# q and k of the first batch: loads by GpSimd's queue, with the cast to f16 in the transfer

## The chip, the cores and the metric

The kernel runs on one core of a Trainium2 chip. The metric is the device time of one execution in microseconds (us). The engines are named as the profile names them: PE is TensorE (PEld its weight loads), DVE is VectorE, ACT is ScalarE, POOL is GpSimd, and SP is SyncE, whose queue (SPq) issues nearly all transfers.

## What is computed

Sliding-window causal attention over 8 batches, 8 heads, 576 positions and 64 values a head, and behind it a gated MLP with a spatial mix. Cut to what matters:

```python
def _attn_ref(q, k, v):                       # each (8, 8, 576, 64), f32
    scores = scale * np.matmul(q, k.transpose(0, 1, 3, 2))
    mask = (rel >= 0) & (rel < window)        # window = 64, rel = row - column
    scores = np.where(mask, scores, -1000000000.0)
    attn = np.exp(scores - np.max(scores, axis=-1, keepdims=True))
    attn = attn / (np.sum(attn, axis=-1, keepdims=True) + 1e-09)
    return np.matmul(attn, v)
...
def _moe_ref(x, w_in, w_spatial, b_spatial, w_out):   # x: (8, 576, 512)
    h = np.maximum(x @ w_in, 0.0)
    u, v = h[..., :512], h[..., 512:]
    v_n = (v - mean(v)) / np.sqrt(var(v) + 1e-06)
    v_s = np.einsum('ts,bsd->btd', w_spatial, v_n) + b_spatial[None, :, None]
    return (u * v_s) @ w_out
```

## The kernel before, in words

**The order is written out.** All work is a list of named steps. The text ORDER gives for each step, in the order in which it is issued, its name, its engine and its buffers (`ck0_0:DVE:0` is step ck0_0, on VectorE, into buffer 0 of its kind). Each engine takes its steps in that order and waits only for the data and buffers of the step at its front. DQ is SyncE's queue. A planner's costs stand beside the steps in the code (`("DQ", 0.45)`), but the order no longer depends on them.

**Names.** A digit pair b_g is batch and group; a group is four of the eight heads. For each b and g:

- ldk, ldq (L412): load of k or q, 128 rows of 1152 f32 values (576 KB), by SyncE, into a buffer of kind "nat" (nk, nq in the profile).
- ck, cq (L416, carried out at L292, L295 or L300): the cast to f16 into a buffer of kind "hqk" (hk, hq), on ACT, DVE or POOL; POOL does it in three parts.
- tk, tq (L419): the transpose of that tile by VectorE, which gives kT and qT.
- S (L479): the scores on PE. E (L486): the exponential on ACT. M (L489): the mask, a minimum on DVE. Z and N, n (L502, L529, L531): sums and their inverse. P and X (L514, L522): attention times v, and the scaled result x.
- ldv (L433): v in five pieces per group, 128 positions of four heads each (128 KB, runs of 64 f32 values), by SyncE. cv: cast to f16 (hv); sl and su: copies shifted by 64 rows (hs). For batches 0 and 1 cv is in two parts: cv0_10 is batch 0, group 1, part 0, which needs the first two pieces of v of that group. sl0_10 and su0_10 copy its result.
- V, U, G, O and the steps around them: the MLP of a batch, which follows later. W are transposes of w_spatial on PE (L378), which use the identity id16.

**The head.** PE runs matmuls on a scratch tile (the D steps, L862) until there is work. On SyncE's queue the order at the start is ldb (the bias), ldk0_0, ldq0_0, ldk0_1, ldv0_00, ldq0_1, ldv0_10, ldv0_11, ldk1_0, ldv0_12, ldv0_13, ldv0_01, ldq1_0 and so on. The casts of batch 0 are ck0_0, cq0_0 and cq0_1 on VectorE and ck0_1 on ScalarE. On VectorE the order is ck0_0, tk0_0, cq0_0, tq0_0, tk0_1, cq0_1, tq0_1, sl0_10, M0_00, su0_10, M0_01, ck1_0.

**Setup ahead of the steps.** GpSimd makes keep (L244 to L247), from which VectorE makes the mask (L252 to L258, small copies), then the identity id16 (L250, a helper's two instructions), then one row of ones in each of two tiles vn4 (L264), which the spatial mix reads. Its first step of the list is cv0_10.

At the end of the kernel function a loop goes through the ordered list, gives each step its buffers and issues it:

Of the kernel before, what the change touches and what calls it, by code (L numbers as in the profile page):

```python
# [15 lines left out]
BIG = 65504.0  # L16

ORDER = """
D24:PE:0 ldb:DQ:0 D5:PE:1 D21:PE:2 ldk0_0:DQ:1 ck0_0:DVE:0 tk0_0:DVE:0 D18:PE:3 D2:PE:2 D14:PE:2
D19:PE:3 D10:PE:0 ldq0_0:DQ:2 ldk0_1:DQ:3 ldv0_00:DQ:0 ldq0_1:DQ:4 ldv0_10:DQ:1 D3:PE:3 ldv0_11:DQ  # L20
cv0_10:POOL:0 ldk1_0:DQ:5 ck0_1:ACT:1 ldv0_12:DQ ldv0_13:DQ ldv0_01:DQ cq0_0:DVE:2 ldq1_0:DQ:6
tq0_0:DVE:1 ldv0_02:DQ D1:PE:2 S0_0:PE:0:1 tk0_1:DVE:2 D22:PE:0 E0_01:ACT:0 E0_00:ACT:1 cq0_1:DVE:3
tq0_1:DVE:3 D15:PE:3 D6:PE:1 D0:PE:2 D26:PE:0 D23:PE:3 S0_r:PE:1:0 E0_r0:ACT:0 E0_r1:ACT cv0_11:POOL
sl0_10:DVE:0 M0_00:DVE ldv0_03:DQ su0_10:DVE M0_01:DVE ck1_0:DVE:0 M0_r:DVE D8:PE:1 Z0_00:PE:2
ldv0_04:DQ ldwin110:DQ:7 ldv0_14:DQ ldwin111:DQ ldwin100:DQ:1 S0_1:PE:1:0 N0_00:ACT:0 E0_11:ACT:2
# [144 lines left out]
class Plan:  # L170
# [3 lines left out]
    def add(self, name, engs, key, fn, deps=(), acq=(), uses=(), mode=None, nbytes=0, n=0):  # L174
        if isinstance(engs, tuple):
            engs = [engs]
        s = Step(name, engs, key, fn, deps, acq, uses, mode, nbytes, n)
        s.n = len(self.steps)
        self.steps.append(s)
        return s  # L180
# [20 lines left out]
def kernel(  # L201
# [11 lines left out]
    nc = tc.nc  # L213
# [19 lines left out]
    def bank(j):  # L233
        return SINGLE[j - 4][:, :]
# [12 lines left out]
    nc.gpsimd.affine_select(out=keep[:], in_=keep[:], compare_op=ALU.is_ge, fill=0.0,  # L247
                            base=64, channel_multiplier=-1, pattern=[[1, 64]])
    id16 = cpool.tile([128, 128], f16, name="id16")
    make_identity(nc, id16[:])  # L250
    mask = cpool.tile([128, 2, 8, 64], f16, name="mask")
    nc.vector.tensor_copy(mask[:, 0, 1, :], keep[:])  # L252
    nc.vector.tensor_scalar(mask[0:64, 0, 0, :], keep[0:64, :], -1.0, BIG, ALU.mult, ALU.add)
# [5 lines left out]
    NSB = 2  # L259
    mv_t = [cpool.tile([128, 5, 2], f32, name=f"mv{i}") for i in range(NSB)]  # L260
    vn4_t = [cpool.tile([65, 512], f16, name=f"vn4_{i}") for i in range(NSB)]
    for i in range(NSB):
        nc.vector.memset(mv_t[i][:], 1.0)
        nc.gpsimd.memset(vn4_t[i][64:65, :], 1.0)  # L264
    w_in_sb = [cpool.tile([128, 1024], f16, name=f"win{r}") for r in range(4)]
    w_out_sb = [cpool.tile([128, 512], f16, name=f"wout{r}") for r in range(4)]
    wspT = [cpool.tile([128, 576], f16, name=f"wspT{kk}") for kk in range(5)]
# [11 lines left out]
    def buf(tag, name):  # L279
        b = Buf(tag, name)  # L280
        if tag in SHAPES:
            shape, d = SHAPES[tag]
            b.make = lambda i: pool.tile(shape, d, tag=f"{tag}_{i}", bufs=1, name=name)
        return b

    plan = Plan()
    add = plan.add
    ENG = {"ACT": nc.scalar, "DVE": nc.vector, "POOL": nc.gpsimd, "PE": nc.tensor, "DQ": nc.sync}

    def cp(e, o, i):  # L290
        if e == "ACT":
            nc.scalar.copy(o, i)  # L292
        elif e == "POOL" and len(i.shape) == 2 and i.shape[1] > 1000:
            for n in (0, 384, 768):
                nc.gpsimd.tensor_copy(o[:, n:n + 384], i[:, n:n + 384])  # L295
        elif e == "POOL" and len(i.shape) == 4 and i.shape[1] > 2:
            for lo, hi in ((0, 2), (2, i.shape[1])):
                nc.gpsimd.tensor_copy(o[:, lo:hi, :, :], i[:, lo:hi, :, :])  # L298
        else:
            ENG[e].tensor_copy(o, i)  # L300

    def cost(n, a=True, d=True, p=True, d1=False):

        out = []
        if a:
            out.append(("ACT", 0.09 + 0.00083 * n))
        if d:
            out.append(("DVE", 0.07 + (0.00104 if d1 else 0.00053) * n))
        if p:
            out.append(("POOL", 0.14 + 0.00083 * n))  # L310
        return out
# [95 lines left out]
    def load_steps(b, g, key):  # L407
        early = b < 2

        def one(name, src, key):  # L410
            n = buf("nat", f"n{name}{b}_{g}")
            ld = add(f"ld{name}{b}_{g}", ("DQ", 0.45), key, lambda e: nc.sync.dma_start(  # L412
                n.t[:, :], src[b, 4 * g:4 * g + 4, :, :].rearrange("h (i j) d -> (h i) (j d)", j=18)),
                acq=[n], nbytes=1.57, n=128)
            h = buf("hqk", f"h{name}{b}_{g}")
            c = add(f"c{name}{b}_{g}", cost(1152), key,  # L416
                    lambda e: cp(e, h.t[:, :], n.t[:, :]), deps=[ld], acq=[h], uses=[n])
            qt = buf("qkT", f"{name}T{b}_{g}")
            d = add(f"t{name}{b}_{g}", ("DVE", 1.09), key, lambda e: nc.vector.transpose(  # L419
                qt.t[:, :].rearrange("p (i j) -> p j i", j=18),  # L420
                h.t[:, :].bitcast(f32).rearrange("p (j w) -> p j w", w=32)),
                deps=[c], acq=[qt], uses=[h])
            return qt, d

        KT[b, g], DKT[b, g] = one("k", k, key)
        QT[b, g], DQT[b, g] = one("q", q, key + 0.001)
        nv = buf("natv", f"nv{b}_{g}")
        lds = []
        for c in range(5):
            sn = 128 if c < 4 else 64  # L430
            lds.append(add(f"ldv{b}_{g}{c}", ("DQ", 0.42),
                           key + 0.002 + 0.0001 * c,
                           lambda e, c=c, sn=sn: nc.sync.dma_start(  # L433
                               nv.t[0:sn, c, :, :],
                               v[b, 4 * g:4 * g + 4, 128 * c:128 * c + sn, :].transpose([1, 0, 2])),
                           deps=lds[-1:], acq=[] if c else [nv], uses=[nv] if c else [],
                           nbytes=0.0051 * sn, n=4 * sn))
        hv = buf("hv", f"hv{b}_{g}")
        hs = buf("hs", f"hs{b}_{g}")
        parts = [(0, 2), (2, 4)] if early else [(0, 4)]  # L440
        done = []
        for n, (lo, hi) in enumerate(parts):
            w = hi - lo
            l0 = max(lo, 1)
            c = add(f"cv{b}_{g}{n}", cost(256 * w), key + 0.003,
                    lambda e, lo=lo, hi=hi: cp(e, hv.t[:, lo:hi, :, :], nv.t[:, lo:hi, :, :]),
                    deps=[lds[hi - 1]] + done[:1], acq=[hv] if n == 0 else [],
                    uses=[nv] + ([hv] if n else []))
            sl = add(f"sl{b}_{g}{n}", cost(256 * (hi - l0)), key + 0.0035,
                     lambda e, l0=l0, hi=hi: cp(e, hs.t[64:128, l0:hi, :, :], hv.t[0:64, l0:hi, :, :]),  # L450
                     deps=[c] + done[1:2], acq=[hs] if n == 0 else [],
                     uses=[hv] + ([hs] if n else []))
            su = add(f"su{b}_{g}{n}", cost(256 * w), key + 0.0035,
                     lambda e, lo=lo, hi=hi: cp(e, hs.t[0:64, lo + 1:hi + 1, :, :],
                                                hv.t[64:128, lo:hi, :, :]),
                     deps=[c, sl if n == 0 else done[1]], uses=[hv, hs])
            done += [c, sl, su]
        done.append(add(f"s4{b}_{g}", cost(256), key + 0.004, lambda e: cp(
            e, hs.t[64:128, 4, :, :], nv.t[0:64, 4, :, :]), deps=[lds[4], done[1]], uses=[nv, hs]))
        HV[b, g], HS[b, g] = hv, hs  # L460
        DHV[b, g] = done
# [417 lines left out]
    for s, eng, banks in CHOOSE(plan):  # L879
        for x in s.acq:  # L880
            if x.tag == "bank":
                x.t = bank(banks.pop(0))
            elif x.tag == "pair":
                x.t = PAIR[banks.pop(0)]
            else:
                x.t = x.make(banks.pop(0))
        s.fn(eng)


# [28 lines left out]
```

## Time and profile before

| | |
|---|---|
| timed runs | 195.65, 195.79, 197.39 us; median 195.79 |
| profiled execution | span 193.6 us from the first to the last instruction; its time outside the span is not listed, the median of the runs is 2.19 us longer |
| granted clock of PE | 1.000 |
| busy, share of the span | PE 95%, DVE 85%, ACT 81%, POOL 45% |
| moved by DMA | 42.73 MB; from HBM 32.79 MB read, to it 9.44 MB written |

How to read it: times in rows are microseconds from the start of the span. A row of a timeline gives the start, the length, the engine, the line of the code, the operation, the tile written and the tiles read with their shapes, a count, and in brackets how long the engine stood idle before it and what ended the wait. A transfer's row on SPq is the issuing alone; the bytes move later, and "DMA to landing" gives the time from the issue until its completion was seen.

### The profile page before, as it was taken

What the parts mean: (1) busy time and instruction counts of PE and PEld (TensorE: products, weight loads), DVE (VectorE), ACT (ScalarE), POOL (GpSimd) and SP (SyncE); (2) the same over time, 40 slices, a digit from 0 to 9 for tenths busy, and PEclk for the clock granted to TensorE, in tenths of its full rate; (3) what the DMA queues carried; (4) which work ended last, traced back from release to release, by engine and by line L of the source; (5) the groups of instructions that cost most, each with busy time, mean ns of one, the idle gap of its engine ahead of it and who ended that gap; (6) DMA issues with size and microseconds to landing.
All of it is one profiled execution on the core that took longest, in us unless ns stands there. A gap on an engine that the chain in (4) does not pass through costs nothing.

```text
span 193.6 us, 7606 instructions
## 1 busy us (share of the span) xinstructions
PE 184.9 (95%) x3218; PEld 107.0 (55%) x3218; DVE 163.7 (85%) x304; ACT 157.1 (81%) x282; POOL 87.4 (45%) x161
## 2 busy tenths in 40 slices
PE   7798998999999999999999999999999999999991
PEld 2352534556556664656665656565756565665560
DVE  4899899999999999998999999998996967468331
ACT  2269998998999999899979999999999875706430
POOL 4027775849932986701956577615641520000000
PEclk9999999999999999999999999999999999999999
DMA  5999999899989997619987999669958000600445
GB/s 177 373 316 290 391 355 333 168 275 373 242 205 332 261 335 179 149 38 289 367 230 184 310 310 282 196 177 218 306 125 266 22 3 0 224 30 0 135 166 191
DMA packets 50421, 42.73 MB, mean 221 GB/s; under 512 B 39377, under 2 KB 39761, under 8 KB 50386
## 3 DMA queue, kind: packets, MB, share of 16 engines
q1 hardware_dynamic: 50162, 42.04, 73.3%
q8 instruction: 25, 0.41, 0.9%
q10 hardware_dynamic: 224, 0.20, 0.3%
q14 instruction: 10, 0.08, 0.1%
HBM read 32.79 MB, written 9.44 MB: 218 GB/s over the span
## 4 chain that ended last, share of the span: by engine, by line
PE 70%; DVE 13%; ACT 9%; DMA 3%; issue 2%; SPq 1%
PE bank L617 50%; PE bank L614 4%; PE pair L479 4%; PE bank L514 3%; DMA nk<-in_k_dram 3%; PE bank L502 3%; ACT e L486 3%; DVE qT L419 2%; PE bank L702 2%; DVE e L489 2%; DVE kT L419 2%; DVE st L671 2%; DVE g L797 1%; DVE x L522 1%; ACT lz L529 1%
## 5 line engine op out<-in xcount | busy, mean ns | idle before, releaser
L617 PE MATMUL bank<-wspT,vn 128*64 128x512 f16 (+3 forms) x530 | 39.1, 296 | 0.0
L486 ACT ACTIVATE e<-pair 128x1024 f16<-128x1024 f32 x32 | 32.0, 1030 | 1.6 <-PE pair L479 1.4
L797 DVE TENSOR_TENSOR g<-bank,ru 128x512 f16<-128x512 f32 (+1 forms) x36 | 23.3, 654 | 9.4 <-PE bank L617 7.0
L647 ACT COPY ob<-bank 128x512 f32<-128x512 f32 (+1 forms) x38 | 21.9, 591 | 9.7 <-PE bank L617 8.4
L669 ACT ACTIVATE vs<-bank 128x512 f16<-128x512 f32 (+1 forms) x40 | 23.8, 602 | 7.1 <-PE bank L705 5.6
L617 PE MATMUL bank<-x,win 128*64 128x512 f16 (+2 forms) x304 | 29.1, 327 | 0.0
L617 PEld LDWEIGHTS <-vn 128*64 128x64 f16 (+1 forms) x530 | 20.8, 111 | 13.2 <-issue 0.2
L671 DVE BATCH_NORM_STATS2 st<-vs 128x6 f32<-128x512 f16 (+1 forms) x40 | 26.0, 670 | 2.3 <-ACT vs L669 2.2
L298 POOL COPY hs<-hv 64x512 f16<-64x512 f16 (+1 forms) x36 | 20.1, 585 | 16.3 <-ACT hv L292 8.4
L617 PE MATMUL bank<-win,x 128*64 128x512 f16 x216 | 27.0, 379 | 0.0
L617 PE MATMUL bank<-wout,g 128*64 128x512 f16 (+1 forms) x208 | 24.7, 371 | 0.0
L522 DVE TENSOR_TENSOR x<-bank,lz 128x512 f16<-128x512 f32 x32 | 21.2, 684 | 3.5 <-PE bank L514 2.2
L489 DVE TENSOR_TENSOR e<-e,mask 128x1024 f16<-128x1024 f16 x32 | 23.0, 725 | 0.5 <-ACT e L486 0.4
L763 ACT ACTIVATE ru<-bank 128x512 f32<-128x512 f32 (+1 forms) x38 | 21.6, 584 | 1.5 <-PE bank L617 0.8
L295 POOL CAST hk<-nk 128x384 f16<-128x384 f32 x36 | 19.4, 574 | 7.1 <-DMA nk<-in_k_dram 6.7
L529 ACT ACTIVATE lz<-bank 128x512 f32<-128x512 f32 x32 | 19.0, 599 | 1.9 <-PE bank L502 1.6
L298 POOL CAST hv<-nv 128x512 f16<-128x512 f32 x18 | 11.7, 661 | 18.8 <-DMA nv<-in_v_dram 18.7
L419 DVE STREAM_TRANSPOSE kT<-hk 128x576 f32<-128x576 f32 x16 | 19.9, 1241 | 0.2 <-ACT hk L292 0.2
L419 DVE STREAM_TRANSPOSE qT<-hq 128x576 f32<-128x576 f32 x16 | 19.8, 1237 | 0.2
L531 ACT ACTIVATE lz<-lz 128x512 f32<-128x512 f32 x32 | 19.6, 642 | 0.0
L295 POOL CAST hq<-nq 128x384 f16<-128x384 f32 x27 | 14.9, 588 | 10.3 <-DMA nq<-in_q_dram 7.8
L617 PEld LDWEIGHTS <-win 128*64 128x64 f16 x304 | 14.4, 110 | 9.2
(91 smaller groups left out, 298.9 us busy)
## 6 DMA issues: line engine op xcount, KB each, us to landing
nk<-in_k_dram SPq DMA_DIRECT2D x16, 576.0 KB, 6.6
nq<-in_q_dram SPq DMA_DIRECT2D x16, 576.0 KB, 6.1
nv<-in_v_dram SPq DMA_DIRECT2D x64, 128.0 KB, 5.9
out_dram<-ob SPq DMA_DIRECT2D x14, 512.0 KB, 5.8
wi<-in_moe_w_in_dram SPq DMA_DIRECT2D x8, 256.0 KB, 5.8
ws<-in_moe_w_spatial_dram SPq DMA_DIRECT2D x4, 288.0 KB, 7.6
nv<-in_v_dram SPq DMA_DIRECT2D x16, 64.0 KB, 4.5
wo<-in_moe_w_out_dram SPq DMA_DIRECT2D x4, 256.0 KB, 7.2
```

The lines of the kernel that those rows point to most:

```text
L295: nc.gpsimd.tensor_copy(o[:, n:n + 384], i[:, n:n + 384])
L298: nc.gpsimd.tensor_copy(o[:, lo:hi, :, :], i[:, lo:hi, :, :])
L419: d = add(f"t{name}{b}_{g}", ("DVE", 1.09), key, lambda e: nc.vector.transpose(qt.t[:, :].rearrange("p (i j) -> p j i", j=18), h.t[:, :].b ...
L486: ex = add(f"E{b}_{g}{u}", ("ACT", 0.91), key, lambda e, u=u: nc.scalar.activation(e2[u].t[:, :, :], sc[u].t[:, :, :], AF.Exp, bias=0.0, s ...
L489: mins.append(add(f"M{b}_{g}{u}", ("DVE", 0.65), key, lambda e, u=u: nc.vector.tensor_tensor(e2[u].t[:, :, :], e2[u].t[:, :, :], mask[:, : ...
L522: lambda e, u=u, ob=ob, lz=lz: nc.vector.tensor_tensor(x.t[:, u, :], ob.t[:, :], lz.t[:, :], ALU.mult),
L617: nc.tensor.matmul(o[c:c + 64, :], w[:, c:c + 64], x, start=start, stop=stop)
L647: lambda e: (nc.vector.tensor_copy if last else nc.scalar.copy)(view(), m.t[rows, 0:n]),
L669: rl = add(f"Vr{b}_{j}", ("ACT", 0.49), key, lambda e: nc.scalar.activation(vs.t[0:jn, :], m.t[0:jn, :], AF.Relu), deps=[pv], acq=[vs], us ...
L671: s1 = add(f"Vb{b}_{j}", ("DVE", 0.6), key + 0.02, lambda e: nc.vector.bn_stats(st6.t[0:jn, 0:6], vs.t[0:jn, :]), deps=[rl], acq=[st6], us ...
L763: lambda e, m=m, ru=ru, n=n: nc.scalar.activation(ru.t[:, 0:n], m.t[:, 0:n], AF.Relu), deps=[pu], acq=[ru], uses=[m])))
L797: nc.vector.tensor_tensor(g.t[:, 0:n], m.t[:, 0:n], ru.t[:, 0:n], ALU.mult)
```

## The change

The loads of q and k of batch 0 (four of 576 KB) move from SyncE's queue to GpSimd's, and write f16 straight into the "hqk" tiles: the cast is part of the transfer. The four cast steps of batch 0 and their f32 buffers are gone. In ORDER the four loads stand at the front (k of group 0, q of group 0, k of group 1, q of group 1). GpSimd's identity and its two memsets of vn4 are issued behind the fourth of them instead of ahead of the list; keep stays ahead. The order of all other steps is as before.

```diff
--- before.py
+++ after.py
@@ -16,10 +16,10 @@
 BIG = 65504.0
 
 ORDER = """
-D24:PE:0 ldb:DQ:0 D5:PE:1 D21:PE:2 ldk0_0:DQ:1 ck0_0:DVE:0 tk0_0:DVE:0 D18:PE:3 D2:PE:2 D14:PE:2
-D19:PE:3 D10:PE:0 ldq0_0:DQ:2 ldk0_1:DQ:3 ldv0_00:DQ:0 ldq0_1:DQ:4 ldv0_10:DQ:1 D3:PE:3 ldv0_11:DQ
-cv0_10:POOL:0 ldk1_0:DQ:5 ck0_1:ACT:1 ldv0_12:DQ ldv0_13:DQ ldv0_01:DQ cq0_0:DVE:2 ldq1_0:DQ:6
-tq0_0:DVE:1 ldv0_02:DQ D1:PE:2 S0_0:PE:0:1 tk0_1:DVE:2 D22:PE:0 E0_01:ACT:0 E0_00:ACT:1 cq0_1:DVE:3
+D24:PE:0 ldk0_0:POOL:0 ldq0_0:POOL:2 ldk0_1:POOL:1 ldq0_1:POOL:3 ldb:DQ:0 D5:PE:1 D21:PE:2 tk0_0:DVE:0 D18:PE:3 D2:PE:2 D14:PE:2
+D19:PE:3 D10:PE:0 ldv0_00:DQ:0 ldv0_10:DQ:1 D3:PE:3 ldv0_11:DQ
+cv0_10:POOL:0 ldk1_0:DQ:5 ldv0_12:DQ ldv0_13:DQ ldv0_01:DQ ldq1_0:DQ:6
+tq0_0:DVE:1 ldv0_02:DQ D1:PE:2 S0_0:PE:0:1 tk0_1:DVE:2 D22:PE:0 E0_01:ACT:0 E0_00:ACT:1 
 tq0_1:DVE:3 D15:PE:3 D6:PE:1 D0:PE:2 D26:PE:0 D23:PE:3 S0_r:PE:1:0 E0_r0:ACT:0 E0_r1:ACT cv0_11:POOL
 sl0_10:DVE:0 M0_00:DVE ldv0_03:DQ su0_10:DVE M0_01:DVE ck1_0:DVE:0 M0_r:DVE D8:PE:1 Z0_00:PE:2
 ldv0_04:DQ ldwin110:DQ:7 ldv0_14:DQ ldwin111:DQ ldwin100:DQ:1 S0_1:PE:1:0 N0_00:ACT:0 E0_11:ACT:2
@@ -247,7 +247,6 @@
     nc.gpsimd.affine_select(out=keep[:], in_=keep[:], compare_op=ALU.is_ge, fill=0.0,
                             base=64, channel_multiplier=-1, pattern=[[1, 64]])
     id16 = cpool.tile([128, 128], f16, name="id16")
-    make_identity(nc, id16[:])
     mask = cpool.tile([128, 2, 8, 64], f16, name="mask")
     nc.vector.tensor_copy(mask[:, 0, 1, :], keep[:])
     nc.vector.tensor_scalar(mask[0:64, 0, 0, :], keep[0:64, :], -1.0, BIG, ALU.mult, ALU.add)
@@ -261,7 +260,6 @@
     vn4_t = [cpool.tile([65, 512], f16, name=f"vn4_{i}") for i in range(NSB)]
     for i in range(NSB):
         nc.vector.memset(mv_t[i][:], 1.0)
-        nc.gpsimd.memset(vn4_t[i][64:65, :], 1.0)
     w_in_sb = [cpool.tile([128, 1024], f16, name=f"win{r}") for r in range(4)]
     w_out_sb = [cpool.tile([128, 512], f16, name=f"wout{r}") for r in range(4)]
     wspT = [cpool.tile([128, 576], f16, name=f"wspT{kk}") for kk in range(5)]
@@ -408,13 +406,17 @@
         early = b < 2
 
         def one(name, src, key):
-            n = buf("nat", f"n{name}{b}_{g}")
-            ld = add(f"ld{name}{b}_{g}", ("DQ", 0.45), key, lambda e: nc.sync.dma_start(
-                n.t[:, :], src[b, 4 * g:4 * g + 4, :, :].rearrange("h (i j) d -> (h i) (j d)", j=18)),
-                acq=[n], nbytes=1.57, n=128)
+            view = src[b, 4 * g:4 * g + 4, :, :].rearrange("h (i j) d -> (h i) (j d)", j=18)
             h = buf("hqk", f"h{name}{b}_{g}")
-            c = add(f"c{name}{b}_{g}", cost(1152), key,
-                    lambda e: cp(e, h.t[:, :], n.t[:, :]), deps=[ld], acq=[h], uses=[n])
+            if b == 0:
+                c = add(f"ld{name}{b}_{g}", ("POOL", 1.0), key,
+                        lambda e: nc.gpsimd.dma_start(h.t[:, :], view), acq=[h], nbytes=1.57, n=128)
+            else:
+                n = buf("nat", f"n{name}{b}_{g}")
+                ld = add(f"ld{name}{b}_{g}", ("DQ", 0.45), key, lambda e: nc.sync.dma_start(
+                    n.t[:, :], view), acq=[n], nbytes=1.57, n=128)
+                c = add(f"c{name}{b}_{g}", cost(1152), key,
+                        lambda e: cp(e, h.t[:, :], n.t[:, :]), deps=[ld], acq=[h], uses=[n])
             qt = buf("qkT", f"{name}T{b}_{g}")
             d = add(f"t{name}{b}_{g}", ("DVE", 1.09), key, lambda e: nc.vector.transpose(
                 qt.t[:, :].rearrange("p (i j) -> p j i", j=18),
@@ -885,6 +887,10 @@
             else:
                 x.t = x.make(banks.pop(0))
         s.fn(eng)
+        if s.name == "ldq0_1":
+            make_identity(nc, id16[:])
+            for i in range(NSB):
+                nc.gpsimd.memset(vn4_t[i][64:65, :], 1.0)
 
 
 # ---- launch: one core; inputs and outputs as the reference has them ----
```

## The prediction

> **What bounds the kernel now.** I read the page first, then the windows, the chain of waits, and the timelines of VectorE, SyncE's queue and GpSimd in the first 14 us. The page gives the length:
>
> ```profile
> span 193.6 us, 7606 instructions
> ```
>
> The timed runs have a median of 195.79 us; 2.19 us of that lie around the span, and I add them unchanged. The windows view has the stretch, busy us of PE, PEld, DVE, ACT and POOL (instructions), the granted clock, the busy share of the DMA engines and their GB/s:
>
> ```profile
> 2.00:3.00 1.00, 1.00 (x4) 0.34 (x3) 0.92 (x4) 0.09 (x1) 0.94 (x3) 1.00 0.76 161
> 3.00:4.20 1.20, 1.20 (x4) 0.39 (x3) 0.57 (x4) 0.00 (x0) 0.17 (x1) 1.00 0.98 361
> 4.20:5.66 1.46, 1.46 (x5) 0.59 (x4) 0.40 (x1) 0.00 (x0) 0.00 (x0) 1.00 1.01 395
> 5.66:7.18 1.52, 1.52 (x8) 0.61 (x6) 1.49 (x3) 0.00 (x0) 0.00 (x0) 1.00 1.00 387
> 7.18:9.10 1.92, 0.96 (x5) 0.32 (x4) 1.89 (x3) 0.90 (x1) 0.00 (x0) 1.00 1.08 382
> 9.10:9.95 0.85, 0.69 (x57) 0.65 (x57) 0.67 (x2) 0.25 (x1) 0.00 (x0) 1.00 1.34 309
> 12.55:33.41 20.86, 19.01 (x366) 9.08 (x365) 19.58 (x33) 18.67 (x35) 14.56 (x22) 1.00 1.08 340
> 33.41:193.60 160.19, 155.75 (x2760) 93.41 (x2759) 134.99 (x252) 134.04 (x245) 69.91 (x127) 1.00 0.69 200
> ```
>
> From 33.41 us on TensorE is busy 155.75 of 160.19 us, and from 12.55 to 33.41 us VectorE is busy 19.58 of 20.86 us. So what the head loses or gains arrives at the end nearly whole, and the head alone is changed. In the head the DMA engines are the limit: from 3.00 us their share is about 1.0. The bytes say what passes when. A q or k load is 0.59 MB; 161 x 1.00 + 361 x 1.20 is 0.594 MB, so k of group 0 has passed at 4.20 us. 395 x 1.46 (0.577) brings q of group 0 at 5.66, 387 x 1.52 (0.588) k of group 1 at 7.18, 382 x 1.92 (0.733) one 0.131 MB piece of v and q of group 1 at 9.10, and 309 x 0.85 (0.263) the next two pieces of v at 9.95. Their order is that of SyncE's queue:
>
> ```profile
> 1.21 0.38 SPq L412 DMA_DIRECT2D nk<-in_k_dram  x1
> 1.63 0.43 SPq L412 DMA_DIRECT2D nq<-in_q_dram  x1
> 2.10 0.43 SPq L412 DMA_DIRECT2D nk<-in_k_dram  x1
> 2.57 0.43 SPq L433 DMA_DIRECT2D nv<-in_v_dram  x1
> 3.05 0.92 SPq L412 DMA_DIRECT2D nq<-in_q_dram  x1
> 4.01 1.12 SPq L433 DMA_DIRECT2D nv<-in_v_dram  x2
> ```
>
> The tiles' answers for the first loads of k and of q give the time from issue to landing:
>
> ```profile
> DMA to landing us min/median/max: 4.0/5.1/6.1
> ```
>
> ```profile
> DMA to landing us min/median/max: 5.0/6.1/7.2
> ```
>
> k lands at 1.21 + 4.0 = 5.21 and 2.10 + 6.1 = 8.20, q at 1.63 + 5.0 = 6.63 and 3.05 + 7.2 = 10.25: 1.0 to 1.15 us after the last byte passed. The chain of waits goes through the second k:
>
> ```profile
> 2.10 6.08 DMA nk<-in_k_dram
> 8.18 0.02 issue
> 8.20 1.16 ACT hk L292
> ```
>
> and then through VectorE's timeline:
>
> ```profile
> 5.26 0.76 DVE L300 CAST hk<-nk 128x1152 f16<-128x1152 f32 x1 [1.66 <-DMA nk<-in_k_dram]
> 6.06 1.26 DVE L419 STREAM_TRANSPOSE kT<-hk 128x576 f32<-128x576 f32 x1
> 7.16 0.75 DVE L300 CAST hq<-nq 128x1152 f16<-128x1152 f32 x1
> 7.95 1.26 DVE L419 STREAM_TRANSPOSE qT<-hq 128x576 f32<-128x576 f32 x1
> 9.38 1.26 DVE L419 STREAM_TRANSPOSE kT<-hk 128x576 f32<-128x576 f32 x1 [0.18 <-ACT hk L292]
> 10.49 0.74 DVE L300 CAST hq<-nq 128x1152 f16<-128x1152 f32 x1
> 11.27 1.26 DVE L419 STREAM_TRANSPOSE qT<-hq 128x576 f32<-128x576 f32 x1
> 12.55 0.22 DVE L300 COPY hs<-hv 64x256 f16<-64x256 f16 x1
> 12.81 0.69 DVE L489 TENSOR_TENSOR e<-e,mask 128x1024 f16<-128x1024 f16 x1
> ```
>
> The reader is to see two things. The four transposes end at 12.53 and everything on VectorE follows without a gap. And the next instruction, the copy hs (step sl0_10), stands ahead of the first mask step M0_00, though it needs v and not q or k.
>
> **The change part by part.** GpSimd's timeline:
>
> ```profile
> 1.34 0.24 POOL L247 TENSOR_SCALAR_AFFINE_SELECT keep<-keep 128x64 f16<-128x64 f16 x1
> 1.52 0.20 POOL masks.py:197 MEMSET id<- 128x128 f16 x1
> 1.79 0.29 POOL masks.py:199 TENSOR_SCALAR_AFFINE_SELECT id<-id 128x128 f16<-128x128 f16 x1
> 2.14 1.03 POOL L264 MEMSET vn<- 1x512 f16 x2
> 11.50 0.61 POOL L300 CAST hv<-nv 128x512 f16<-128x512 f32 x1 [8.33 <-DMA nv<-in_v_dram]
> ```
>
> *Moved setup.* The identity and the two memsets (1.52 to 3.17, so 1.65 us) go behind four transfers. They cost nothing: GpSimd idles 8.33 us before the cast of v at 11.50, and the identity's first reader is late:
>
> ```profile
> 35.48 2.39 PE L378 MATMUL bank<-id,wn 128*128 128x128 f16 x25
> ```
>
> Without that cover they would cost their 1.65 us. VectorE's mask waits for keep, which stays in front.
>
> *Issuing by GpSimd.* No row shows it. Below it is bounded by SyncE's 0.38 us for the same load; above by one pass of GpSimd over such a tile, three casts:
>
> ```profile
> 17.10 1.90 POOL L295 CAST hq<-nq 128x384 f16<-128x384 f32 x3 [1.02 <-DVE e L489]
> ```
>
> I take 1.0 us, near the middle, which is also what the diff enters for the planner. Keep is done at 1.58, so the four issues end at 2.6, 3.6, 4.6 and 5.6. SyncE's first k was issued by 1.59 and its bytes begin at 2.0, 0.4 later; so GpSimd's bytes begin at 3.0, not at 2.0. The Trainium skill, DMA: Bandwidth & Descriptors, section Latency and other measured facts, gives the first byte as about 1 us on GpSimd's path and 0.6 us on SyncE's; with that extra 0.4 us in place of my 1.0 the loads would begin at 2.4 and nothing below would change, because v decides.
>
> *SyncE's queue loses four loads.* The v pieces, behind three or four 0.59 MB loads until now, come first. The DMA engines have the same bytes to move and stay full: in 2.0 to 3.0 the 0.161 MB that k had now go to v.
>
> *Sharing.* From 3.0 on two queues feed the same engines. I take one row of k or q (4608 B) in turn with one packet of v (256 B, one head of one position), at the 385 GB/s of the middle rows: k and q get 4608 of 4864 parts, 365 GB/s, 1.62 us a load, and pass at 4.62, 6.24, 7.86 and 9.48. The other ends, SyncE's queue getting nothing or half, are 1.53 and 3.06 us a load. Landed, with 1.0, 1.0, 1.0 and 1.15 us: 5.62, 7.24, 8.86, 10.63.
>
> *Casts removed.* They go from VectorE (0.76, 0.75, 0.74) and ScalarE (1.16). The transposes then run 5.62 to 6.88, 7.24 to 8.50, 8.86 to 10.12 and 10.63 to 11.89 instead of ending at 12.53: 0.64 us earlier. The first scores start near 8.5 instead of:
>
> ```profile
> 9.26 0.67 PE L479 MATMUL pair<-qT,kT 32*128 32x128 f16 x56 [1.12 <-DVE qT L419]
> ```
>
> *What is late next: v.* hs needs the cast at 11.50, which waits for the second piece of v of group 1, the third piece in all. Of 0.393 MB, 0.161 pass by 3.0, 0.131 in turn with the 32 rows per engine, and the last 0.101 at 309 GB/s in 0.33 us: 9.81 instead of 9.95. With the lag of before (11.50 - 9.95 = 1.55) the cast starts at 11.36, ends at 11.97, and hs starts at about 12.0 instead of 12.55. Behind hs on VectorE stands M0_00, behind that on TensorE the sums and the next scores, and behind those ScalarE's work. So of 1.76 us of casts on the chain (1.16, and 0.60 between 10.64 and 11.24) only 0.55 us come out.
>
> **Sum:** 195.79 - 0.55 = 195.24, say 195.2 us (span 193.0). Its own range is 194.4 to 196.2.
>
> **The rivals.** *GpSimd's issuing is late.* The loads hold the gain as long as the last lands by 12.53 - 1.26 = 11.27; with an issue of g, 1.58 + 4g + 0.4 + 1.62 + 1.15 passes that at g = 1.63. At 1.90 it lands at 12.35 and the transposes end at 13.61, 1.08 us late: 196.9. A second way there is that VectorE's mask copies hold GpSimd off:
>
> ```profile
> 2.75 0.49 DVE L257 COPY mask<-mask 128x192 f16<-128x192 f16 x1
> 3.27 0.29 DVE L258 COPY mask<-mask 128x512 f16<-128x512 f16 x1
> ```
>
> The smaller copy, while GpSimd's memsets ran (2.14 to 3.17), took 0.49 us and the larger one, alone, 0.29: the two engines do disturb each other. If the first issue starts only at 3.56, the bytes begin at 4.96, the four loads pass at 11.44, land at 12.6, and the transposes end at 13.85: 1.3 us late, 197.1. Against it: the copies have gaps, and end at 3.56. The Trainium skill, SBUF — State Buffer, section Who interferes with whom, states this as a rule: a VectorE copy in a two-port mode blocks GpSimd wholly, and with it the writing of descriptors. By that rule the time is the 197.1; the stretched copy agrees with a disturbance, not with its size.
>
> *Equal shares in bytes* (the rival on the other side). If SyncE's queue, filled with v and the next batch's k, gets half of 385 GB/s, a load takes 3.06 us, the fourth passes at 15.26, lands at 16.4 and the transposes end at 17.7, 5.1 us late: 200.9. It turns slower once the four loads need more than 11.27 - 1.15 - 3.0 = 7.1 us, under 332 GB/s, 86% of the engines. For it: SyncE's queue holds 4608 B rows too, behind the v pieces. Against: 96 small v packets per engine come before them, and the four loads have 32 rows per engine. The Trainium skill, DMA: Bandwidth & Descriptors, section Queues, rings and completion order, has the engines change between queues packet by packet; read on one-row packets that is my sum, read on packets filled to equal size it is this rival. No row of before can tell, since one queue did all.
>
> *The cast halves the transfer's rate.* Same price, 200.9; nothing in the trace shows a cast in a transfer, and the change would then remove casts from idle engines to slow the bound one.
>
> *The whole saving.* If v passes early and a load that writes half its bytes costs the engines less, all 1.76 us come out: 194.0. It needs the fourth load by 9.5 us. Against it: 0.59 MB are still read, and the share is 1.0 already.
>
> **How the numbers follow.** Forecast 0.50, late issuing 0.18, equal shares 0.12, a slow cast 0.06, the whole saving 0.14. The range reaches up over late issuing and the milder forms of unequal sharing to 199.0, which leaves out about 0.12, and down to 194.0, which leaves out about 0.07. A measurement of this kernel tells about 1% (1.96 us) from no change. Faster by that, under 193.8: half of the whole saving and a little of the forecast's tail and of luck behind the head, 0.11. Slower, over 197.75: both heavy cases and a tail of the third, 0.21. Between: 0.68.
>
> **What would show it.** Right: a GpSimd queue with four issues near 1.0 us from about 1.6; no casts of hk and hq before 14 us; first scores at 8.3 to 8.9; the last transpose before 12.0; hs waiting for GpSimd's cast of v and starting near 12.0; the same 0.5 us at 33 us and at the end. Wrong: the fourth load landing after 11.3 us (late issuing if its issue is late, sharing or a slow cast if its bytes are), v landing well before 11, or a head gain that is gone at the end.

## The result and the profile after

| | before | after |
|---|---|---|
| median of 15 runs each, us | 195.81 | 197.54 |
| ratio, 95% interval | | 1.007 (1.0042 to 1.0098) |
| span of the profiled execution, us | 193.6 | 195.7 |
| landings of k0, q0, k1, q1 (digit: group), us | 5.2, 6.6, 8.2, 10.25 | 6.8, 8.3, 11.2, 12.8 |
| last transpose ends, hs starts, us | 12.53, 12.55 | 14.09, 14.11 |

The change is slower by 0.7%; the forecast was 195.2 us. The ratio is not the quotient of the medians, which would be 1.009: the means of the runs, 196.06 us before and 197.45 after, are 1.39 us apart, the medians 1.73 us. From the page of the changed kernel, the span, and the new queue with its packets, MB and share of the engines:

```profile
span 195.7 us, 7605 instructions
...
q0 software_dynamic: 576, 1.18, 3.2%
```

The four loads are 576 packets, 144 each (128 rows and 16 more), and are counted at the 1.18 MB they write, half of what they read. GpSimd's timeline:

```profile
1.52 0.67 POOL L413 DMA_DIRECT2D hk<-in_k_dram  x1
2.19 0.54 POOL L413 DMA_DIRECT2D hq<-in_q_dram  x1
2.71 0.59 POOL L413 DMA_DIRECT2D hk<-in_k_dram  x1
3.29 0.54 POOL L413 DMA_DIRECT2D hq<-in_q_dram  x1
...
11.92 0.61 POOL L298 CAST hv<-nv 128x512 f16<-128x512 f32 x1 [6.47 <-DMA nv<-in_v_dram]
```

The issues take little more than half of what was assumed and are over at 3.83. SyncE, free of four loads, begins to issue v at 1.23, ahead of GpSimd's first load, and issues the next batch's k at 2.78, ahead of GpSimd's fourth:

```profile
1.23 1.51 SPq L435 DMA_DIRECT2D nv<-in_v_dram  x3
2.78 0.52 SPq L416 DMA_DIRECT2D nk<-in_k_dram  x1
```

From issue to landing, first for hk and then for hq (minimum, median, maximum of two loads of each after the change):

```profile
DMA to landing us min/median/max: 5.3/6.9/8.5
```

```profile
DMA to landing us min/median/max: 6.1/7.8/9.5
```

So k lands at 1.52 + 5.3 = 6.8 and 2.71 + 8.5 = 11.2, q at 2.19 + 6.1 = 8.3 and 3.29 + 9.5 = 12.8. The windows view, with three of the prediction's windows:

```profile
2.00:3.00 1.00, 1.00 (x4) 0.35 (x3) 0.88 (x5) 0.10 (x1) 1.00 (x3) 1.00 0.54 123
3.00:4.20 1.20, 1.20 (x4) 0.41 (x3) 0.21 (x3) 0.00 (x0) 1.12 (x4) 1.00 0.65 116
5.66:7.18 1.52, 1.52 (x6) 0.56 (x5) 0.29 (x1) 0.00 (x0) 0.00 (x0) 1.00 1.06 195
```

Before, the share of the DMA engines was 0.76 from 2.00 to 3.00 and 0.98 from 3.00 to 4.20; now it is 0.54 and 0.65. Then it is full, and GB/s reads low only because cast rows count at half. VectorE's timeline has none of batch 0's casts left, and in their place four waits for transfers:

```profile
6.89 1.26 DVE L421 STREAM_TRANSPOSE kT<-hk 128x576 f32<-128x576 f32 x1 [3.68 <-DMA hk<-in_k_dram]
8.35 1.26 DVE L421 STREAM_TRANSPOSE qT<-hq 128x576 f32<-128x576 f32 x1 [0.20 <-DMA hq<-in_q_dram]
11.26 1.25 DVE L421 STREAM_TRANSPOSE kT<-hk 128x576 f32<-128x576 f32 x1 [1.65 <-DMA hk<-in_k_dram]
12.83 1.26 DVE L421 STREAM_TRANSPOSE qT<-hq 128x576 f32<-128x576 f32 x1 [0.31 <-DMA hq<-in_q_dram]
14.11 0.22 DVE L298 COPY hs<-hv 64x256 f16<-64x256 f16 x1
14.37 0.69 DVE L491 TENSOR_TENSOR e<-e,mask 128x1024 f16<-128x1024 f16 x1
```

The chain of waits names the fourth load:

```profile
3.29 9.51 DMA hq<-in_q_dram
12.80 0.02 issue
12.83 1.27 DVE qT L421
```

hs starts 1.56 us later than before. At 33 us the same sums on TensorE start 1.70 us later, first before the change, then after it:

```profile
33.41 0.41 PE L502 MATMUL bank<-e,ones 128*64 128x512 f16 x2 [0.24 <-DVE e L489]
...
35.11 0.41 PE L504 MATMUL bank<-e,ones 128*64 128x512 f16 x2 [0.24 <-DVE e L491]
```

The median is 1.73 us longer. The loss is made by 14 us and kept.

### The profile page after: what moved, and what is told of

Its sections match the earlier page's. It is cut to its first block, busy times and chain, and to the rows that moved or that the text cites. A ratio compares the mean times of both kernels' runs of the same rounds, so it can differ in the third digit from the quotient of the medians.

```text
span 195.7 us, 7605 instructions
## 1 busy us (share of the span) xinstructions
PE 185.5 (95%) x3218; PEld 107.2 (55%) x3218; DVE 161.0 (82%) x301; ACT 155.9 (80%) x281; POOL 92.2 (47%) x165
## 3 DMA queue, kind: packets, MB, share of 16 engines
q0 software_dynamic: 576, 1.18, 3.2%
## 4 chain that ended last, share of the span: by engine, by line
PE 78%; ACT 7%; DVE 5%; DMA 5%; issue 1%; POOL 1%; POOLq 0%
PE bank L619 53%; PE bank L616 8%; DMA hq<-in_q_dram 5%; PE pair L481 4%; PE bank L516 4%; PE bank L504 3%; ACT e L488 3%; PE bank L704 3%; DVE st L673 1%; ACT hs L290 1%; DVE qT L421 1%; ACT lz L533 1%; ACT lz L531 1%; PE bank L376 1%; DVE e L491 1%
## 5 line engine op out<-in xcount | busy, mean ns | idle before, releaser
L491 DVE TENSOR_TENSOR e<-e,mask 128x1024 f16<-128x1024 f16 x32 | 24.7, 776 | 0.3 <-ACT e L488 0.3
L293 POOL CAST hk<-nk 128x384 f16<-128x384 f32 x36 | 20.5, 604 | 4.5 <-DMA nk<-in_k_dram 4.3
```

The lines of the kernel that those rows point to most:

```text
L491: mins.append(add(f"M{b}_{g}{u}", ("DVE", 0.65), key, lambda e, u=u: nc.vector.tensor_tensor(e2[u].t[:, :, :], e2[u].t[:, :, :], mask[:, : ...
```

## The experiments

The theory formed from these traces: **the four loads lost their place.** In one queue the order of issue is a priority; in two queues v and the next k of SyncE share the engines with q and k of batch 0. The rivals: the cast makes the transfer slow; GpSimd issues late or is held off by VectorE's copies; the moved setup costs. Each experiment was compared with the kernel before on the same chip.

### The four loads alone: e1_gate and e5_gate_nocast

SyncE's queue is held behind a small copy out of the fourth tile, so the four loads have the engines to themselves; e5 does the same with f32 loads and the casts on chip. So v comes late in both, and what is read is the landings, not the times.

```diff
-... ldq0_1:POOL:3 ldb:DQ:0 D5:PE:1 ...
+... ldq0_1:POOL:3 ldb:DQ:0 gate:DQ:9 D5:PE:1 ...
+    add("gate", ("DQ", 0.4), -1.0, lambda e: nc.sync.dma_start(
+        gt.t[:, 0:256], GATED["q", 1].t[:, 0:256]), acq=[gt])
```

> The changed kernel, but SyncE issues nothing behind the bias until q of group 1 has landed (a small copy of that tile on its queue waits for it), so GpSimd's four loads have the DMA engines to themselves; the whole time is not the point, since v comes late. Landings of k0, q0, k1, q1 were 6.8, 8.3, 11.2 and 12.8 us in the changed kernel. Sharing (SyncE's packets slow the four loads): 5.6 to 6.0, then 1.5 us apart, the fourth by 10.5. GpSimd's path itself (late first bytes, late completions): the first still at 6.4 to 6.8, then 1.5 apart or more, the fourth at 11.2 to 12. A slow cast: 2 us or more apart even alone, the fourth at 12.5 or later.

> The first experiment (SyncE held until q of group 1 has landed) with f32 loads and the casts on chip: the four loads alone on the engines, without the cast. So far the fourth landed at 10.6 us alone with the cast, 12.8 shared with it, 11.4 shared without it. If the cast costs engine time by itself, the fourth lands at about 9.2 (10.6 less the 1.4 of the shared pair) and the spacing shrinks. If the cast costs only in turn with SyncE's packets, it lands at 10.2 to 10.6 as with the cast. The whole time tells nothing.

Landing of hq in e1 (the 2.0 is the gate's own copy), then of nq in e5 (1.9 is the gate):

```profile
DMA to landing us min/median/max: 2.0/5.1/7.3
```

```profile
DMA to landing us min/median/max: 1.9/5.1/7.0
```

In e1 the fourth load lands at 3.29 + 7.3 = 10.6, where the prediction had it (10.63) with v beside it; in e5 at 3.23 + 7.0 = 10.2. Alone, neither GpSimd's queue nor the cast is slow: the cast costs 0.4 us in four loads (one execution of each) and does not halve the rate. The times, 200.21 and 200.68 us (one run each), hold v's delay (hs waits until 16.36 and 15.86) and a stretch of half clock (last section).

### With sharing, without the cast: e2_nocast

```diff
-ldk0_0:POOL:0 ldq0_0:POOL:2 ldk0_1:POOL:1 ldq0_1:POOL:3 ...
+ldk0_0:POOL:1 ldq0_0:POOL:2 ldk0_1:POOL:3 ldq0_1:POOL:4 ...   (f32, into "nat")
+ck0_0:DVE:0 ... ck0_1:ACT:1 ... cq0_0:DVE:2 ... cq0_1:DVE:3   (as before)
```

> The changed kernel with f32 loads by GpSimd's queue and the four casts back on VectorE and ScalarE: the queue alone is changed, not the cast. Sharing and GpSimd's path both expect the same landings as in the changed kernel within 0.4 us (6.8, 8.3, 11.2, 12.8), the last transpose at about 15.6 instead of 14.1 us, and about 199.0 us. A slow cast expects the fourth landing at 11.8 or earlier and about 198 us or less.

Measured 199.89 us, ratio 1.0183 (1.0151 to 1.0215). Landing of nq:

```profile
DMA to landing us min/median/max: 6.1/7.2/8.2
```

The fourth lands at 3.23 + 8.2 = 11.4. That is the landing that a slow cast had expected (11.8 or earlier), without its time (198 or less); e5 above was built to tell, and alone the cast costs little. Fourth landings, all four cases:

| | SyncE held back | SyncE sharing |
|---|---|---|
| f32 | 10.2 (e5) | 11.4 (e2) |
| f16, cast in the transfer | 10.6 (e1) | 12.8 (the change) |

Sharing costs 1.2 us without the cast and 2.2 with it. The view of the DMA queues, taken for one us at a time, shows how (packets, MB, share of the 16 engines). From 8 to 9 us in e2:

```profile
q0 software_dynamic: 91, 0.38, 93.1%
q1 hardware_dynamic: 91, 0.02, 10.2%
```

One 256 B packet of v for each row of k or q, as the prediction took it (98 to 97 and 90 to 91 in the us around it). In the changed kernel, from 3 to 4 us and then from 10 to 11:

```profile
q1 hardware_dynamic: 302, 0.08, 33.2%
q0 software_dynamic: 10, 0.02, 18.2%
...
q0 software_dynamic: 66, 0.13, 66.5%
q1 hardware_dynamic: 135, 0.14, 44.5%
```

and alone, in e1, from 3 to 4 us:

```profile
q0 software_dynamic: 60, 0.14, 84.9%
```

Packets of GpSimd's queue in each us, from the same view:

| us | 2 | 3 | 4 | 5 | 6 | 7 | 8 | 9 | 10 | 11 | 12 |
|---|---|---|---|---|---|---|---|---|---|---|---|
| the change | 0 | 10 | 65 | 87 | 82 | 77 | 81 | 78 | 66 | 25 | 5 |
| e1, alone | 9 | 60 | 87 | 95 | 93 | 90 | 99 | 40 | 3 | | |
| e2, shared, f32 | 0 | 5 | 56 | 93 | 89 | 98 | 91 | 90 | 54 | | |
| e12, alone until 9 | 6 | 61 | 86 | 97 | 89 | 79 | 79 | 64 | 15 | | |
| e8, shared, issued 0.2 us earlier | 12 | 69 | 57 | 75 | 81 | 59 | 65 | 64 | 57 | 36 | 1 |

In the change and in e2 GpSimd's rows start about a us later than alone. In e8, further down, they do not, although v is issued ahead of them there as well. With the cast and sharing there is also a long end: 96 packets are left at 10 us and need more than two us, while SyncE's queue moves 0.14 MB in one us, 1 KB a packet, so rows of the next k are already among them.

### Only the next k held back: e6_gate_next

```diff
-... D3:PE:3 ldv0_11:DQ
+... D3:PE:3 ldv0_11:DQ gate:DQ:9     (gate: a copy out of k of group 1)
```

> The changed kernel, but SyncE waits behind the first three pieces of v until k of group 1 has landed, so only v shares the engines with the four loads, not the next batch's k. If v's small packets delay them, the landings stay at 6.8, 8.3, 11.2 and 12.8 within 0.3 us and the time is 197.5 to 198.5. If the next k's large rows do, the third and fourth land by 9.8 and 11.3, the last transpose ends by 12.6 and the time is 195.6 to 196.4.

Measured 197.88 us, ratio 1.0068 (1.0033 to 1.0103). VectorE's last transpose:

```profile
12.17 1.26 DVE L423 STREAM_TRANSPOSE qT<-hq 128x576 f32<-128x576 f32 x1 [0.43 <-DMA hq<-in_q_dram]
```

The fourth load lands 0.6 us earlier than in the change (12.2, third 10.5 instead of 11.2), between the two expectations. With the next k the gate holds back the pieces of v behind it too. And the first two loads land 0.6 us later than in the change (7.4 and 8.9), though nothing ahead of them differs: 0.6 us is also what two executions can differ by, so the next k's part is not shown more closely than that. The time is no better: the next cast on VectorE waits for that k (0.49 us at 15.92), and TensorE runs 3.4 us at half clock (last section).

### Only the start undisturbed: e12_gate_start

```diff
-        gt.t[:, 0:256], GATED["q", 1].t[:, 0:256]), acq=[gt])    (e1)
+        gt.t[:, 0:256], GATED["k", 0].t[:, 0:256]), acq=[gt])
```

> The changed kernel with one thing added: SyncE's queue is held until k of group 0 has landed, so that GpSimd's queue has the engines to itself at its start and shares them only afterwards. In the changed kernel 10 rows of GpSimd's queue pass in 3 to 4 us beside v, alone it was 60. If this late start is a term of its own (0.9 us of the 2.2 by which the fourth load misses the forecast), the first load lands at 5.9 us as when alone, and the fourth at 11.4 to 12.0 instead of 12.8. If only the sum of the bytes ahead counts, the fourth lands at 12.8 again. In both cases v starts 5 us later, and at about one 256 B packet of v for each row of k or q its second piece of group 1 does not land before the fourth load: the cast of v then starts after 12.8 us, the copy behind it after 13.4, and the time stays near 197 to 197.7 us, so that the start alone saves nothing.

Measured 197.61 us, ratio 1.0109 (1.0052 to 1.0166). VectorE:

```profile
10.98 1.26 DVE L423 STREAM_TRANSPOSE qT<-hq 128x576 f32<-128x576 f32 x1 [0.23 <-DMA hq<-in_q_dram]
13.62 0.22 DVE L298 COPY hs<-hv 64x256 f16<-64x256 f16 x1 [1.38 <-POOL hv L298]
```

The time, the cast of v (12.97) and hs fall where expected; the fourth load, at 11.0, came earlier than the 11.4 to 12.0. The reason was not foreseen: SyncE issues v from 6.44 on, but from 6 to 9 us its queue passes nothing, not even the gate's own copy, issued at 5.84. From 6 to 7:

```profile
q0 software_dynamic: 89, 0.17, 108.1%
```

There is no row of q1. Here the queue that comes second waits until the first is nearly empty. So this run does not isolate the start as meant; it shows that whoever is served first delays the other, k and q here by v or v by k and q, and that both are needed by 12 us.

### Another second queue: e3_actq

The four loads as f32 on ScalarE's queue, casts on chip as before.

```diff
+            ld = add(f"ld{name}{b}_{g}", ("ACT", 1.0) if far else ("DQ", 0.45), key,
+                     lambda e: (nc.scalar if far else nc.sync).dma_start(n.t[:, :], view), ...)
```

> The four loads f32 by ScalarE's hardware queue, casts on chip as before: two queues share the engines, but neither is GpSimd's. Sharing: the landings are as late as in the changed kernel (fourth at 12 to 13), and with the casts 198.5 to 199.5 us. GpSimd's path: landings as in the kernel before within about 1 us (fourth by 11.3), 195.8 to 196.8 us.

Measured 198.48 us, ratio 1.0118 (1.0072 to 1.0165), with landings at 4.9, 6.8, 8.9 and 12.4. The queue's own timeline:

```profile
1.74 0.47 ACTq L414 DMA_DIRECT2D nk<-in_k_dram  x1
4.92 0.34 ACTq L414 DMA_DIRECT2D nq<-in_q_dram  x1
```

Time is lost here without GpSimd and without a cast in the transfer, but the run does not show that sharing lost it. The first three loads land within 0.7 us of where they landed before; only the fourth is late, by 2.2 us, and it was issued only when the first had landed, 1.9 us later than before (4.92 against 3.05).

### The loads ahead of everything: e8_first

GpSimd's four issues ahead of keep, so that VectorE's mask copies, which need keep, run after the issuing.

```diff
-    nc.gpsimd.memset(keep[:], BIG)     (and the rest of keep and mask, ahead of the list)
+        if s.name == "ldq0_1":
+            nc.gpsimd.memset(keep[:], BIG)     (and the rest, behind the fourth load)
```

> The changed kernel with GpSimd's four loads ahead of keep as well, and so VectorE's mask copies behind GpSimd's issuing. If the copies held GpSimd off, each issue shrinks from 0.54 to 0.67 us to 0.45 or less and the landings come more than 0.7 us earlier. If they did not, the issues last as long, all landings move by the 0.7 us of the earlier issue (6.1, 7.6, 10.5, 12.1) and the time is 196.6 to 197.0. If sharing alone sets the fourth landing, it moves by less than 0.3 us and the time stays at 197.3 or more.

Measured 198.19 us, ratio 1.0091 (1.0053 to 1.0129). GpSimd's first and last issue:

```profile
1.31 0.67 POOL L401 DMA_DIRECT2D hk<-in_k_dram  x1 [0.79 <-POOLq L908]
...
3.01 0.57 POOL L401 DMA_DIRECT2D hq<-in_q_dram  x1
```

With no copy of VectorE beside them the issues take 0.67, 0.55, 0.56 and 0.57 us, in the change 0.67, 0.54, 0.59 and 0.54: the copies do not hold GpSimd off. Issued 0.2 to 0.3 us earlier, the first lands at 5.8 instead of 6.8, but the third and fourth land at 10.9 and 12.6, hardly earlier, as was expected if sharing alone sets the fourth. The queues from 3 to 4 us:

```profile
q0 software_dynamic: 69, 0.16, 100.7%
q1 hardware_dynamic: 18, 0.00, 1.9%
```

So the late start is not what decides. By 4.0 us e8 has passed 81 packets, the change 10; by 10 us they have passed 482 and 480. What e8 wins at the start it loses again beside what SyncE's queue sends later.

VectorE's copies beside GpSimd do show a disturbance, the other way round: the copy of 128x128 takes 0.48 us beside GpSimd's memsets of vn4 (before the change and in e8), and 0.20 us beside the issues of the change.

### Only group 1 moved: e4_group1

k and q of group 0 stay first in SyncE's queue with their casts on VectorE; group 1 goes by GpSimd with the cast.

```diff
-            if b == 0:
+            if b == 0 and g == 1:
```

> Only q and k of group 1 by GpSimd's queue with the cast; group 0 first on SyncE's queue with its casts on VectorE. GpSimd's path: group 0 lands near 5.5 and 7.5, group 1, issued 1.2 us earlier than in the changed kernel and with two loads ahead instead of none on its own queue, at 9 to 11; last transpose at 11.8 to 12.4, 195.2 to 196.0 us. Sharing: group 0 is delayed by group 1's rows in turn with it, to 6.5 and 9 or later, last transpose at 12.6 to 13.2, 196.0 to 196.8 us.

Measured 195.02 us, ratio 0.9947 (0.9916 to 0.9978): faster than before by half a per cent. The queues from 4 to 5 us, where q0 has no row, and from 6 to 7:

```profile
q1 hardware_dynamic: 103, 0.41, 101.1%
...
q0 software_dynamic: 80, 0.18, 94.3%
q1 hardware_dynamic: 72, 0.02, 14.1%
```

SyncE's k and q, issued first, pass first and land at 5.2 and 6.6, as before the change; the delay to 6.5 and 9 that was expected of sharing does not come. Then group 1 passes with about one packet of v in turn (72 packets are 0.02 MB, so there is no next k among them), and lands at 8.1 and 9.8. VectorE:

```profile
10.10 1.24 DVE L421 STREAM_TRANSPOSE qT<-hq 128x576 f32<-128x576 f32 x1
12.06 0.22 DVE L298 COPY hs<-hv 64x256 f16<-64x256 f16 x1 [0.72 <-POOL hv L298]
12.31 0.69 DVE L491 TENSOR_TENSOR e<-e,mask 128x1024 f16<-128x1024 f16 x1
```

The transposes end at 11.34 and hs waits for the cast of v (11.41) until 12.06. The wait for v and the start of hs are those that the prediction had for the whole change (cast at 11.36, hs at 12.0).

### Queue or casts: e11_group1_nocast

The same without the cast in the transfer.

```diff
+            far = b == 0 and g == 1
+            ld = add(f"ld{name}{b}_{g}", ("POOL", 1.0) if far else ("DQ", 0.45), key, ...)
+            c = add(f"c{name}{b}_{g}", ...)     (as before)
```

> The version with only group 1's k and q by GpSimd (195.02 us), but as f32, cast on chip as in the kernel before. It separates the second queue from the missing casts. If the gain is that VectorE and ScalarE no longer cast group 1 (1.0 us or so ahead of the last transposes), the last transpose ends at 12.2 to 12.6 us as before and the time goes back to 195.6 to 196.3 us. If the gain comes from the second queue alone, it stays at 195.0 us.

Measured 195.66 us, ratio 0.9971 (0.9943 to 0.9998). VectorE:

```profile
11.24 1.26 DVE L419 STREAM_TRANSPOSE qT<-hq 128x576 f32<-128x576 f32 x1
12.53 0.22 DVE L298 COPY hs<-hv 64x256 f16<-64x256 f16 x1
```

Time and transposes are those expected if the missing casts make e4's gain. The intervals of e4 and e11 overlap, so the times alone do not settle it; the timelines do for the head (hs 12.06 against 12.53).

### What comes after the wait for v: e7_vorder, e9_mask_first, e10_before_mask_first

e7 is e4 with the two v pieces of group 1 ahead of that of group 0; e9 is e4, and e10 the kernel before, with M0_00 ahead of sl0_10.

```diff
-D19:PE:3 D10:PE:0 ldv0_00:DQ:0 ldv0_10:DQ:1 D3:PE:3 ldv0_11:DQ
+D19:PE:3 D10:PE:0 ldv0_10:DQ:1 ldv0_11:DQ ldv0_00:DQ:0 D3:PE:3     (e7)
-sl0_10:DVE:0 M0_00:DVE ldv0_03:DQ ...
+M0_00:DVE sl0_10:DVE:0 ldv0_03:DQ ...     (e9, e10)
```

> The kernel with group 1 alone on GpSimd's queue, and on SyncE's queue the two pieces of v of group 1 ahead of the piece of group 0. There VectorE stood 0.72 us idle ahead of hs (12.06), waiting for v. If v is what decides, hs starts at 11.4 to 11.6 and the time falls by about 0.5 us to 194.3 to 194.8. If something behind it decides (the next mask step waiting for its exponential, later loads), the time stays at 195.0.

> The version with only group 1's k and q by GpSimd with the cast (195.02 us), with one swap in VectorE's order: the first mask multiply M0_00 goes ahead of the slice product sl0_10. If what ends the wait at 12 us is only the cast of v in front of sl0_10, M0_00 no longer stands behind it: it starts when its exponential is done, about 11.95 us instead of 12.31, and the time falls by 0.36 us, to 194.6 to 194.7. If the later use of the slice product on TensorE sets the pace instead, the time stays at 195.0.

> The kernel before with the same one swap and nothing else, as a control: M0_00 ahead of sl0_10 on VectorE. If only M0_00's place in the order counts, it starts at 12.55 us instead of 12.81 and the time falls by 0.26 us, to about 195.5. If the slice product is needed as early, no change: 195.8.

e7: 195.08 us, 0.9946 (0.9915 to 0.9977). e9: 195.24 us, 0.9951 (0.9917 to 0.9985). Both are e4's time; of e7 only the times are used. e10: 195.78 us, 0.9968 (0.9936 to 0.9999). The interval holds the 0.26 us of one expectation and ends next to no change, the other, so it decides nothing. VectorE in e9:

```profile
11.92 0.69 DVE L491 TENSOR_TENSOR e<-e,mask 128x1024 f16<-128x1024 f16 x1 [0.61 <-ACT e L488]
12.65 0.52 DVE L298 COPY hs<-hv 64x256 f16<-64x256 f16 x2
```

The mask starts 0.39 us earlier than in e4, hs 0.59 later, and the time stays: the order of those two is not what limits the kernel there. In e7 the time stays too, with v ordered earlier; whether hs starts earlier there is not shown. So the wait for v at 12 us is real in e4, but that it sets the end is not shown.

## Why the prediction was wrong, point by point

The time lies inside the stated range, 194.0 to 199.0 us, but on the other side of the kernel before, and the range had been drawn up to 199.0 for rivals, not for the forecast. Of the signs named for being wrong, one came: the fourth load lands after 11.3 us, at 12.80, and its issue is early.

**What bounds the kernel: right.** 1.56 us lost at hs arrive as 1.73 at the end. The prediction's lag from landing to the end held as well: its turning point was a fourth landing at 11.27; 12.80 is 1.53 past it, and 195.79 + 1.53 = 197.3 against 197.54 measured.

**Moved setup: right.** GpSimd is done with it at 5.45 and idles 6.47 us before the cast of v.

**Issuing by GpSimd: too dear, without effect.** 0.54 to 0.67 us instead of 1.0. The start of the bytes at 3.0 was right for the queue alone, but by luck: in e1 the first rows pass at about 2.9, because the shorter issue (over at 2.19) is followed by a longer wait for the bytes, 0.7 us instead of 0.4. The 0.4 itself was misread: SyncE's k, issued by 1.59, shows its first packets at 2.2 in the view of the queues before the change, not at 2.0. Late issuing, the rival with 0.18 and 197.1 us, has nearly the time but not the cause: the last issue is over at 3.83 instead of 5.6, and VectorE's copies do nothing to it (e8). The Trainium skill, SBUF — State Buffer, section Who interferes with whom, has a VectorE copy in a two-port mode block GpSimd wholly; no blocking is seen in these rows, which do not show the mode the copies ran in.

**Sharing: the step that failed.** It had the loads pass from 3.0 on at 1.62 us each, or 89 packets a us, beside one packet of v a row, and land by 10.63. That landing is what they reach alone (e1). With SyncE's queue beside them they miss it by 2.2 us, and the packets of the one profiled execution say at which time they fall behind. *Start:* at 4.0 us 10 packets have passed, not 89; 79 at 89 a us are 0.89 us. Two queues were assumed to share at once and to keep the engines full; the engines are not full (0.65 from 3.00 to 4.20, and 0.25 from 3.4 to 3.8), so v in front of them does not explain it, and why the rows start late stays open. *Rate:* from 4 to 10 us 470 packets pass, not 533: 0.71 us. *End:* 96 are left at 10; at 89 a us they would pass at 11.08 and land at 12.23 instead of 12.80: 0.57 us. The sum is 2.17. At the end the next k is in play, which the forecast left out though it stood in the rival: with it and what is behind it held back, the fourth lands 0.6 us earlier (e6).

The three terms are a count, not three causes: e8 has no late start and lands at 12.6 all the same. What is shown as the cause is the whole: SyncE's queue beside the four loads costs them 2.2 us. It does not gain by it either: the third piece of v is issued by 2.74 instead of 5.13, and still its cast starts at 11.92 instead of 11.50. The turn of packet by row itself was right (e2: 91 and 91), and this also agrees with the Trainium skill, DMA: Bandwidth & Descriptors, section Queues, rings and completion order, read on one-row packets; the quiet queue of e12 does not fit that reading.

So the rival on the other side, equal shares in bytes, was right in sign and place and far too heavy in size (200.9): from 4 to 11 us SyncE's queue moved 0.42 MB beside some 2.2 MB of k and q.

**The cast's rate.** Not halved (e1, e5). It costs 0.4 us alone and 1.4 when shared (12.8 against 11.4). Why the second is more, the runs do not show: 77 to 81 packets a us with v beside them, but also 79 in e12 where nothing shares, against 90 and 99 in e1.

**Casts removed: right, and of no use here.** They are gone from VectorE, but with the loads late the engine waits in their place. Where the loads keep their time (e4) hs starts 0.49 us earlier than before (12.06 against 12.55), near the 0.55 us to be had; the ratio gives 0.4 to 1.6 us for the whole kernel.

**v decides: right for hs, not shown for the end.** In e4, hs waits for the cast of v, within 0.1 us of the forecast, but with v ordered earlier (e7) or the mask taken from behind hs (e9) the time stays. In the change v is cast at 11.92 (forecast 11.36) and the fourth load decides.

## What to carry to other kernels

Loads in one queue have an order, and that order is a priority. Before moving the most urgent ones to another queue, list what the first queue will then send in their place and what it will take from engines that are already full. A cast in the transfer pays when the cast is on the path and the load is not the one the head waits for: here for the second pair of loads moved alone, and not for all four. The first pair alone was not tried.

## What was not expected of the hardware

**The second queue often waits.** GpSimd's rows behind SyncE's k and q (none from 4 to 5 us in e4), v behind GpSimd's rows (none from 6 to 9 us in e12, 18 from 3 to 4 us in e8): there the queue whose bytes began later got little or nothing for a us or more. It is no rule: in e2 the two queues pass one packet each in turn from 6 us on, and in e3 both pass side by side from 3 us on. What hands out the turns was not tried.

**The clock falls after a wait.** In e2 TensorE stood idle before its first scores:

```profile
10.91 0.73 PE L479 MATMUL pair<-qT,kT 32*128 32x128 f16 x56 [3.57 <-DVE qT L419]
```

and the windows after it give the granted clock (third number from the right):

```profile
11.00:12.00 1.00, 1.00 (x58) 0.64 (x58) 0.93 (x1) 0.35 (x2) 0.17 (x1) 0.67 1.01 389
12.00:13.00 1.00, 1.00 (x4) 0.43 (x3) 1.00 (x2) 1.00 (x2) 0.45 (x1) 0.50 1.19 276
```

With 0.50 until 14 and 0.62 from 14 to 15, the half clock lasts 0.66 + 2 + 0.76 = 3.4 us. It also came in e6 after 2.70 us idle and in e3 after 2.06 and another 0.50 us (3.4 us long each), and in e1 and e5 around waits of 4.54 and 2.70 us (6.8 us long each), but not in e5 after an earlier 2.01 us, in e8 after 1.69 us or in the changed kernel (1.13 us). The Trainium skill, TensorE: Matmul & The Clock Gate, section Part 1: The HAM clock gate (the "warmup" mystery), gives windows of about 3.4 us for both directions: the duration agrees (twice that in e1 and e5), while less idling was enough here: 2.70 us (e6), or 2.06 and 0.50 us (e3). So the times of e1, e2, e3, e5 and e6 hold a share for the clock, and their landings, not their times, carry the argument above.
